# Two interleaved transformer layers on one core: layer B moved to one step behind layer A, lag 2 in place of 3

## The chip, the core and the metric

The kernel runs on one core of a Trainium2 chip. The metric is device time in microseconds (us), the median of the runs. Five engines work side by side, each with its own queue that is worked off in order: PE (TensorE, matmuls, with its weight loads as PEld), DVE (VectorE), ACT (ScalarE), POOL (GpSimd) and SP (SyncE), which here only issues DMAs. Work on different engines is ordered by semaphores: an instruction at the head of a queue that waits holds up everything behind it on that engine.

## The reference

The input x has 2048 rows of 640 values. Four layers follow each other, A B A B, each added to x, each on a layer norm of x. Both A layers share one set of weights, both B layers another.

```python
def _A_ref(x, mem0, Wq, Wk, Wv, Wo, seg_len):      # 32 heads of 192, 64 segments of 32 rows
    mem = mem0                                       # 8 memory rows
    for s in range(n_seg):
        xs = x[:, s * seg_len:(s + 1) * seg_len, :]
        h = jnp.concatenate([mem, xs], axis=1)       # 40 rows
        q = jnp.einsum('btd,dhe->bhte', h, Wq)       # likewise k, v
        scores = jnp.einsum('bhqe,bhke->bhqk', q, k) * scale
        p = _softmax(jnp.where(mask[None, None], scores, -1e9), axis=-1)
        o = jnp.einsum('bhte,hed->btd', jnp.einsum('bhqk,bhke->bhqe', p, v), Wo)
        mem = o[:, :M, :]                            # goes into the next segment
        outs.append(o[:, M:, :])

def _B_ref(x, wqkv, wo):                             # 32 heads of 20, window of 8 at distance 2
    kg = k[:, :, idx_c, :]; vg = v[:, :, idx_c, :]   # rows pos, pos-2, ..., pos-14
    attn = _softmax(jnp.where(mask, jnp.einsum('bhsd,bhswd->bhsw', q, kg) * scale, -1e9))
    return jnp.einsum('bhsw,bhswd->bhsd', attn, vg).reshape(B, S, D) @ wo

x = x + _A_ref(_layernorm(x), A_mem0, ...)
x = x + _B_ref(_layernorm(x), B_wqkv, B_wo)
x = x + _A_ref(_layernorm(x), A_mem0, ...)
x = x + _B_ref(_layernorm(x), B_wqkv, B_wo)
```

Layer A is a recurrence over 64 segments: the memory rows that a segment gives enter the next one. A B segment needs its own 32 rows and the 14 rows before them.

## The kernel before

**Steps and lanes.** The 64 segments are worked in steps. Two lanes lie side by side in every tile: lane 0 is the first A layer on segment t, lane 1 the second A layer on segment t - LAG. Each lane has 40 columns (8 memory, 32 input), so a matmul of layer A has 80 moving columns where both lanes are at work. LAG is 3: steps 0 to 2 have lane 0 alone, steps 3 to 63 both (61 steps), steps 64 to 66 lane 1 alone. In these one-lane steps the matmuls have 40 columns (`set_lanes`, `cols`). Layer B of both lanes runs behind: `step(t)` does the first part of B for b1 = t - 1 (layer norm, K, Q, V and the transposed V) and the second for b2 = t - 2 (scores, P.V, output). So two more steps, 67 and 68, hold B alone. The result of B's lane 0 goes into `xin` and is lane 1's input of the next step; lane 1's goes into `YT` and out.

**A step of layer A.** 32 heads are worked in 8 quads of four heads. For each quad PE projects K (`a_k`, 30 matmuls), Q (`a_q`, 30) and V (`a_v`, 10 matmuls of 384 columns), then P.V of the quad before (`a_pv`, 8), the output projection `a_o` of the quad two before (30 matmuls, added up over all quads in one PSUM tile, `acc`), and the scores (`a_s`, 8). ACT copies K out of PSUM into KF and Kz, takes the exponentials and the reciprocal of the softmax sums (as exp of minus log, tile R). DVE copies Q (QT) and V (Vt, after the P.V that read the old Vt), masks the exponentials (Em) and scales the output of P.V (OT, three instructions, `a_norm`). At the end of a step follow `a_o(5)`, `a_o(6)` and `a_o(7)`; then `mem_out` (DVE) copies the memory columns of acc into hT, the input of the next step's first `a_k`, and `b_x1` forms x1, the input of layer B. Between `a_o(7)` and the next step's first `a_k` stand `b_q` and `b_vt` of layer B (35 matmuls). PSUM gives the projections four buffers in turn (`ps_big`), each free again once its copy is done.

**Weights.** Layer A's weights are 64 pieces of 480 KB ("halves"). They don't fit: 34 stay in SBUF, 30 are read from HBM again in every step, through a ring of six buffers on SP's queue. `half_order` gives the order in which PE needs the halves, `resident_halves` which of them stay (every so-many-th by count). POOL loads layer B's weights (`load_b_weights`), builds its masks at step 1 (`build_masks_b`), expands Q by heads (`b_qexp`, tile QX, against a mask `hmask` of 128x384) and moves x in and the result out.

**What sets the order.** All of `run` but the prologue stands in a block in which the order of the Python calls is the order on every engine. Nothing is rearranged.

Of the kernel before, what the change touches and what calls it, by code (L numbers as in the profile page):

```python
# [10 lines left out]
BF16 = mybir.dt.bfloat16  # L11
F32 = mybir.dt.float32
ACT = mybir.ActivationFunctionType
ALU = mybir.AluOpType
# [3 lines left out]
P = 128  # L18
D = 640
NC = 5  # L20
# [8 lines left out]
LAG = 3  # L29
# [14 lines left out]
def half_order():  # L44

    order = []
    for i in range(NQUAD - 1):
        order += [("k", i), ("q", i), ("v", i)]
        if i >= 2:
            order.append(("o", i - 2))  # L50
    order += [("k", 7), ("q", 7), ("v", 7), ("o", 5), ("o", 6), ("o", 7)]
    return [(kind, i, h) for kind, i in order for h in range(2)]

def resident_halves():
    res = set()
    for n, u in enumerate(half_order()):
        if (n * N_RES) // N_HALVES != ((n + 1) * N_RES) // N_HALVES:
            res.add(u)
    return res

class Kernel:
    def __init__(self, ctx, tc, A_x, A_mem0, A_Wq, A_Wk, A_Wv, A_Wo, B_wqkv, B_wo, out):
        self.tc = tc
        self.nc = tc.nc
# [12 lines left out]
        self.ebp = pool("ebp", 4)  # L77
        self.xp = pool("xio", 1)
# [47 lines left out]
    def load_b_weights(self, i):  # L126
        if i == 0:
            self.nc.gpsimd.dma_start(out=self.wqkv[:].rearrange("p c n -> p (c n)"), in_=self.B_wqkv)
        else:
            self.nc.gpsimd.dma_start(out=self.wo[:].rearrange("p c n -> p (c n)"), in_=self.B_wo)  # L130
# [15 lines left out]
    def build_masks_b(self):  # L146
        nc, cp = self.nc, self.cp

        def band(name, cur):
            m = cp.tile([P, NX], BF16, name=name)  # L150
            nc.gpsimd.memset(m[:], 0.0)
            for half in range(2):
                off = 0 if half == cur else SEG
                for l in range(2):
                    r0 = 64 * half + SEG * l
                    blk = m[r0:r0 + SEG, SEG * l:SEG * (l + 1)]
                    for w in range(BW):
# [14 lines left out]
        hm = cp.tile([P, BHC, NX], BF16, name="hmask")  # L172
        nc.gpsimd.memset(hm[:], 1.0)
        nc.gpsimd.affine_select(out=hm[:], in_=hm[:], compare_op=ALU.is_ge, fill=0.0, base=0,
                                pattern=[[-BD, BHC], [0, NX]], channel_multiplier=1)
        nc.gpsimd.affine_select(out=hm[:], in_=hm[:], compare_op=ALU.is_ge, fill=0.0, base=BD - 1,
                                pattern=[[BD, BHC], [0, NX]], channel_multiplier=-1)
# [33 lines left out]
    def proj(self, kind, i, t):  # L211

        nc = self.nc
        hT = self.hT[t % 2]
        ps = self.big(f"ps_{kind}")
        for n in range(6):
            if n % 3 == 0:
                w = self.half(kind, i, n // 3)
            for c in range(NC):
                nc.tensor.matmul(ps[:, NT * n + self.c0:NT * n + self.c1], lhsT=w[:, c, P * (n % 3):P * (n % 3 + 1)],  # L220
                                 rhs=hT[:, NT * c + self.c0:NT * c + self.c1],
                                 start=(c == 0), stop=(c == NC - 1))
        return ps
# [29 lines left out]
    def a_v_out(self, out):  # L253

        for pr, ps in enumerate(out):
            src = ps[0:NT, 0:384].rearrange("p (j e) -> p j e", j=2)
            dst = self.Vt[0:NT, 512 * pr:512 * (pr + 1)].rearrange("p (j x) -> p j x", j=2)[:, :, 0:DH]
            self.nc.vector.tensor_copy(out=dst, in_=src)  # L258
# [36 lines left out]
    def a_norm(self, i, split=False):  # L295
        nc = self.nc
        ov, r = self.cols(self.ov), self.cols(self.r[:])
        ot = self.ap2.tile([P, 2, 3, NT], BF16, name="OT")
# [14 lines left out]
    def a_o(self, i):  # L313
# [5 lines left out]
        for m in (0, 2, 3, 5, 1, 4):  # L319
            for c in range(NC):  # L320
                nc.tensor.matmul(self.acc[:, NT * c + self.c0:NT * c + self.c1], lhsT=w[m // 3][:, m % 3, P * c:P * (c + 1)], rhs=self.cols(ot[:, m]),  # L321
                                 start=(i == 0 and m == 0 and c == 0), stop=(i == NQUAD - 1 and m == 4), skip_group_check=True)
# [5 lines left out]
    def mem_out(self, t):  # L328
# [6 lines left out]
        nc.vector.tensor_copy(out=h[:, :, self.l0:self.l1, 0:NM], in_=a[:, :, self.l0:self.l1, 0:NM])  # L335
# [98 lines left out]
    def b_qexp(self, c):  # L434
# [3 lines left out]
                                     in1=self.hmask[:, 0:nh, :], op=ALU.mult)  # L438
# [80 lines left out]
    def prologue(self):  # L519
# [9 lines left out]
        self.build_mask_a()  # L529

    def step(self, t):
        T = self.n_seg + LAG
        self.set_lanes(t)
        b1 = t - 1 if 0 <= t - 1 < T else None
        b2 = t - 2 if 0 <= t - 2 < T else None
        nt = t + 1
        a = t < T
        for i in range(NQUAD - 1):
            if a:
                self.a_k(i, t)  # L540
                self.a_q(i, t)
                ps = self.a_v(i, t)
# [3 lines left out]
                if i >= 2:  # L546
                    self.a_o(i - 2)
            if i == 0 and b1 is not None:
                self.b_ln(b1)
            if b2 is not None and 3 <= i <= 4:  # L550
                self.b_pv(i - 3)
            if a and i >= 1:
                self.a_norm(i - 1)
            if b2 is not None and i == 6:
                self.b_wo(b2)
            if b2 is not None:
                if 1 <= i <= 3:
                    self.b_s(b2, 2 * i - 2)
                    self.b_s(b2, 2 * i - 1)
                if i < 3:  # L560
                    self.b_qexp(2 * i)
                    self.b_qexp(2 * i + 1)
                if i == 5:
                    self.b_ot()
            if i == 3 and b1 is not None:
                self.b_ln_apply(b1)
            if a:
                self.a_s()
            if t == 1 and i in (0, 3):
                self.load_b_weights(i)  # L570
            if t == 1 and i == 4:
                self.build_masks_b()
            if i == 1:
                if nt < self.n_seg:
                    self.x_load(nt)
                yseg = t - 3 - LAG
                if yseg >= 0 and yseg % 4 == 3:
                    self.y_store(yseg // 4)
        if a:
            self.a_k(7, t)  # L580
            self.a_q(7, t)
        if nt < T:
            self.ln1_sq(nt)
        if a:
            self.a_pv()
            self.a_v_out(self.a_v(7, t))
            self.a_norm(6, True)
            self.a_s()
            self.a_norm_mid()
            self.a_o(5)  # L590
        if nt < T:
            self.ln1(nt)
        if a:
            self.a_pv()
        if nt < T:
            self.ln1_rstd()
        if a:
            self.a_norm(7)
            self.a_o(6)
        if nt < T:  # L600
            self.ln1_apply(nt)
        if b1 is not None:
            self.b_v(b1)
            self.b_k(b1)
        if a:
            self.a_o(7)
            if nt < T:
                self.mem_out(t)
            self.b_x1(t)
        if b1 is not None:  # L610
            self.b_q(b1)
            self.b_vt()

    def run(self, ctx):
        self.x1p = ctx.enter_context(self.tc.tile_pool(name="x1p", bufs=2))
# [75 lines left out]
```

## Time and profile before

Three runs took 3385.59, 3378.62 and 3387.4 us: the median is 3385.59 us. The profiled execution took 3381.59 us, with a span of 3379.9 us from the first to the last instruction.

| engine | busy us | share of the span | instructions |
|---|---|---|---|
| PE | 3277.7 | 97% | 72896 |
| PEld | 2877.8 | 85% | 72896 |
| DVE | 2179.0 | 64% | 5966 |
| ACT | 1845.1 | 55% | 5830 |
| POOL | 388.5 | 11% | 575 |

The DMA engines are busy in 85% (SP's queue), at 303 GB/s; the chain that ended last is PE to 91%. In the timeline the first `a_k` of a step marks where the step begins:

| stretch | from | to | us each |
|---|---|---|---|
| before step 0 | 0 | 11.15 | |
| step 0 (lane 0, all 64 halves come for the first time) | 11.15 | 89.19 | 78.0 |
| step 1 (lane 0) | 89.19 | 135.46 | 46.3 |
| step 2 (lane 0) | 135.46 | 183.47 | 48.0 |
| steps 3 to 63 (both lanes) | 183.47 | 3209.59 | 49.6 |
| steps 64 to 66 (lane 1) | 3209.59 | 3345.0 | 45.1 |
| steps 67, 68 (B alone) and the last store | 3345.0 | 3379.9 | |

Read the table by stretch: the 61 two-lane steps are 90% of the span, and what is different in them counts 61 times.

### The profile page before, as it was taken

The numbers are of one execution on the slowest core, as the hardware profiler recorded it, in microseconds if no ns is written. First come the engines' busy times: TensorE is split into PE (matmuls) and PEld (weight loads), VectorE is DVE, ScalarE is ACT, GpSimd is POOL, SyncE is SP. The second block draws the span as 40 slices with busy tenths as digits, with TensorE's granted clock in tenths as the row PEclk, the third lists the DMA queues.
The fourth block names the chain that finished last, engine by engine and source line by source line (L and its number), as shares of the span: only waits on it lengthen the run. The fifth ranks groups of instructions, "written<-read, shape, count | busy, mean of one in ns | idle before, by whom it ended". The sixth has DMA issues, their size and how long they took to land.

```text
span 3379.9 us, 164632 instructions
## 1 busy us (share of the span) xinstructions
PE 3277.7 (97%) x72896; PEld 2877.8 (85%) x72896; DVE 2179.0 (64%) x5966; ACT 1845.1 (55%) x5830; POOL 388.5 (11%) x575
## 2 busy tenths in 40 slices
PE   6899999999999999999999999999999999999987
PEld 4788888888888888888888888888888888888875
DVE  2566666666666666666666666666666666666665
ACT  2455555555555555555555555555555555555543
POOL 0210111011011011101101101110110110111011
PEclk8999999999999999999999999999999999999998
DMA  9988988888888888898888889888988888888894
GB/s 394 359 296 300 309 300 300 309 299 297 302 306 298 299 306 300 300 312 294 302 302 308 297 301 311 299 299 306 306 300 297 305 296 298 309 298 304 300 337 161
DMA packets 298412, 1023.87 MB, mean 303 GB/s; under 512 B 34288, under 2 KB 34288, under 8 KB 297568
## 3 DMA queue, kind: packets, MB, share of 16 engines
q1 hardware_dynamic: 294624, 1004.85, 85.4%
q8 instruction: 570, 9.34, 1.1%
q0 software_dynamic: 3072, 8.48, 0.8%
q14 instruction: 146, 1.20, 0.1%
HBM read 1010.58 MB, written 2.62 MB: 300 GB/s over the span
## 4 chain that ended last, share of the span: by engine, by line
PE 91%; DVE 4%; DMA 3%; issue 1%; POOL 0%; ACT 0%; SPq 0%; POOLq 0%; ACTq 0%
PE ps_v L249 25%; PE ps_k L220 16%; PE ps_q L220 16%; PE ps_acc L321 14%; PE ps_o L286 5%; PE ps_s L267 2%; PE ps_s L268 2%; PE ps_bq L405 2%; PE ps_bk L405 2%; PE ps_bs L445 2%; PE ps_bv L405 1%; PE ps_by L488 1%; DMA w_q<-in_A_Wq_dram 1%; DVE Vt L258 1%; DMA w_ring<-in_A_Wq_dram 1%
## 5 line engine op out<-in xcount | busy, mean ns | idle before, releaser
L290 ACT ACTIVATE R<-ps_o 64x160 f32<-64x160 f32 (+1 forms) x2144 | 627.4, 293 | 926.0 <-issue 512.6
L258 DVE CAST Vt<-ps_v 80x384 bf16<-80x384 f32 x1072 | 557.8, 550 | 402.2 <-PE ps_o L286 331.7
L249 PEld LDWEIGHTS <-hT 128*128 128x128 bf16 x5360 | 494.6, 99 | 293.9 <-issue 13.9
L437 POOL TENSOR_TENSOR QX<-QB,hmask 128x384 bf16<-128x384 bf16 (+1 forms) x402 | 326.2, 832 | 2801.6 <-ACT QB L416 2159.4
L220 PEld LDWEIGHTS <-w_ring 128*128 128x128 bf16 x15075 | 597.1, 100 | 19.0 <-issue 8.7
L249 PE MATMUL ps_v<-w_ring,hT 128*128 128x384 bf16 x2680 | 529.4, 329 | 5.0 <-DMA w_ring<-in_A_Wv_dram 4.9
L249 PE MATMUL ps_v<-w_v,hT 128*128 128x384 bf16 x2680 | 530.6, 329 | 2.4 <-DMA w_v<-in_A_Wv_dram 2.4
L321 PE MATMUL ps_acc<-OT,w_o 128*128 128x80 bf16 (+1 forms) x9045 | 482.5, 200 | 6.6 <-issue 5.2
L238 DVE CAST QT<-ps_q 128x480 bf16<-128x480 f32 (+1 forms) x536 | 340.6, 635 | 226.6 <-PE ps_q L220 208.6
L301 DVE TENSOR_TENSOR OT<-ps_o,R 128x320 bf16<-128x320 f32 (+1 forms) x536 | 254.7, 475 | 318.3 <-ACT R L292 314.2
L220 PE MATMUL ps_q<-hT,w_q 128*128 128x80 bf16 (+1 forms) x9045 | 406.0, 200 | 7.4 <-DMA w_q<-in_A_Wq_dram 4.9
L321 PE MATMUL ps_acc<-OT,w_ring 128*128 128x80 bf16 (+1 forms) x7035 | 399.9, 200 | 2.0 <-DMA w_ring<-in_A_Wo_dram 2.0
L321 PEld LDWEIGHTS <-w_o 128*128 128x128 bf16 x9045 | 381.0, 99 | 7.5 <-issue 5.7
L220 PE MATMUL ps_k<-hT,w_ring 128*128 128x80 bf16 (+1 forms) x8040 | 369.7, 200 | 5.9 <-DMA w_ring<-in_A_Wk_dram 2.6
L220 PE MATMUL ps_k<-hT,w_k 128*128 128x80 bf16 (+1 forms) x8040 | 370.2, 200 | 3.1 <-DMA w_k<-in_A_Wk_dram 2.0
L220 PEld LDWEIGHTS <-w_q 128*128 128x128 bf16 x9045 | 351.3, 100 | 9.0 <-DMA w_q<-in_A_Wq_dram 5.8
L220 PE MATMUL ps_q<-hT,w_ring 128*128 128x80 bf16 (+1 forms) x7035 | 324.8, 200 | 9.7 <-issue 5.0
L220 PEld LDWEIGHTS <-w_k 128*128 128x128 bf16 x8040 | 315.7, 100 | 4.0 <-DMA w_k<-in_A_Wk_dram 2.4
L321 PEld LDWEIGHTS <-w_ring 128*128 128x128 bf16 x7035 | 306.6, 99 | 2.3 <-DMA w_ring<-in_A_Wo_dram 2.3
L231 ACT CAST KF<-ps_k 128x320 bf16<-128x320 f32 (+1 forms) x536 | 220.0, 410 | 160.4 <-PE ps_k L220 159.6
L286 PEld LDWEIGHTS <-Vt 80*128 80x128 bf16 x4288 | 208.9, 98 | 73.4 <-DVE OT L311 20.4
L292 ACT ACTIVATE R<-R 128x320 f32<-128x320 f32 (+1 forms) x536 | 245.7, 458 | 16.9
(94 smaller groups left out, 4049.3 us busy)
## 6 DMA issues: line engine op xcount, KB each, us to landing
w_ring<-in_A_Wk_dram SPq DMA_DIRECT2D x536, 480.0 KB, 5.1
w_ring<-in_A_Wv_dram SPq DMA_DIRECT2D x536, 480.0 KB, 5.0
w_ring<-in_A_Wq_dram SPq DMA_DIRECT2D x469, 480.0 KB, 5.0
w_ring<-in_A_Wo_dram SPq DMA_DIRECT2D x469, 480.0 KB, 5.3
w_q<-in_A_Wq_dram SPq DMA_DIRECT2D x9, 480.0 KB, 9.6
w_o<-in_A_Wo_dram SPq DMA_DIRECT2D x9, 480.0 KB, 9.7
w_k<-in_A_Wk_dram SPq DMA_DIRECT2D x8, 480.0 KB, 9.6
w_v<-in_A_Wv_dram SPq DMA_DIRECT2D x8, 480.0 KB, 9.6
```

Of the source, the lines that this page charges most:

```text
L220: nc.tensor.matmul(ps[:, NT * n + self.c0:NT * n + self.c1], lhsT=w[:, c, P * (n % 3):P * (n % 3 + 1)], rhs=hT[:, NT * c + self.c0:NT * c ...
L231: nc.scalar.copy(out=kf, in_=pv[:, :, 0:3:2, :])
L238: self.nc.vector.tensor_copy(out=self.cols(qt[:]), in_=self.cols(ps[:, 0:6 * NT].rearrange("p (a n) -> p a n", a=6)))
L249: nc.tensor.matmul(ps[:, 0:384], lhsT=hT[:, NT * c:NT * c + P], rhs=w[:, c, :], start=(c == 0), stop=(c == NC - 1))
L258: self.nc.vector.tensor_copy(out=dst, in_=src)
L286: nc.tensor.matmul(self.cols(ov[:, pr, k]), lhsT=vt[0:NT, 512 * pr + c0:512 * pr + c0 + P], rhs=self.cols(em[0:NT, 2 * pr + k // 2]), star ...
L290: nc.scalar.activation(out=self.cols(r[r0:r0 + 64, :, j]), in_=self.cols(src), func=ACT.Ln)
L292: nc.scalar.activation(out=rf, in_=rf, func=ACT.Exp, scale=-1.0)
L301: nc.vector.tensor_tensor(out=oc[:, :, 0:3:2], in0=ov[:, :, 0:4:3], in1=r, op=ALU.mult)
L321: nc.tensor.matmul(self.acc[:, NT * c + self.c0:NT * c + self.c1], lhsT=w[m // 3][:, m % 3, P * c:P * (c + 1)], rhs=self.cols(ot[:, m]), s ...
L405: nc.tensor.matmul(ps[:, NX * n:NX * (n + 1)], lhsT=self.wqkv[:, c, e0:e0 + P], rhs=self.h2T[:, c, :], start=(c == 0), stop=(c == NC - 1))
L437: self.nc.gpsimd.tensor_tensor(out=qx[:, 0:nh, :], in0=self.qb[:, c, :].unsqueeze(1).to_broadcast([P, nh, NX]), in1=self.hmask[:, 0:nh, :] ...
```

## The change

- LAG is 2. Steps 0, 1 and 64, 65 have one lane, steps 2 to 63 both (62 steps); there are 66 A steps, and one step (66) with B alone.
- Layer B runs for one b = t - 1 within step t: layer norm at quad 0, Q and K at 1, V at 2, the transposed V at 3, P.V at 4 and 5, transpose and output at 6; the scores at quads 2 to 4. Nothing of B is left between `a_o(7)` and the next step's first `a_k`.
- The output projection of a quad is four quads behind (OLAG = 4) in place of two: `a_o(i - 4)` from quad 4 on, and `a_o(3)` to `a_o(7)` at the end of the step. OT has four buffers.
- In quad 7 the P.V of quad 6 stands between K and Q (it stood behind Q), and one of the two copies of V goes to ACT.
- The last output projection ends chunk by chunk (all of a 128-row chunk of the output before the next), `mem_out` is two copies (chunks 0 and 1, then 2 to 4), and the first K of a step takes chunk after chunk of its input.
- Which halves stay is chosen by the columns that PE works between them; 34 stay, 30 are read again.
- `wqkv` is loaded after quad 6 of step 0, `wo` after quad 0 of step 1 (each behind a copy of one element of Em, so that the DMA can't start earlier). The masks of B are built in the prologue. `hmask` is 128x6 and is read with a step of 0 along the columns.

```diff
-LAG = 3
+LAG = 2
+OLAG = 4
...
 def resident_halves():
+    order = half_order()
+    whole = sum(n for _, n in order)
+    streamed, at = 0, 0
     res = set()
-    for n, u in enumerate(half_order()):
-        if (n * N_RES) // N_HALVES != ((n + 1) * N_RES) // N_HALVES:
+    for u, n in order:
+        if streamed < N_HALVES - N_RES and at * (N_HALVES - N_RES) >= streamed * whole:
+            streamed += 1
+        else:
             res.add(u)
+        at += n
     return res
...
+    def load_b_weights(self, w, src):
+        self.nc.gpsimd.tensor_copy(out=w[0:1, 0, 0:1], in_=self.em[0:1, 0, 0:1])
+        self.nc.gpsimd.dma_start(out=w[:].rearrange("p c n -> p (c n)"), in_=src)
...
     def proj(self, kind, i, t):
+        w = [self.half(kind, i, h) for h in range(2)]
+        mem_last = kind == "k" and i == 0
+        order = [(n, c) for c in range(NC) for n in range(6)] if mem_last else [(n, c) for n in range(6) for c in range(NC)]
+        for n, c in order:
...
     def a_o(self, i):
+        order = [(m, c) for m in (0, 2, 3, 5, 1, 4) for c in range(NC)]
+        if i == NQUAD - 1:
+            order = [(m, c) for m in (0, 2, 3) for c in range(NC)] + [(m, c) for c in range(NC) for m in (5, 1, 4)]
...
     def mem_out(self, t):
-        nc.vector.tensor_copy(out=h[:, :, self.l0:self.l1, 0:NM], in_=a[:, :, self.l0:self.l1, 0:NM])
+        for cs in (slice(0, 2), slice(2, NC)):
+            nc.vector.tensor_copy(out=h[:, cs, self.l0:self.l1, 0:NM], in_=a[:, cs, self.l0:self.l1, 0:NM])
...
     def b_qexp(self, c):
-                                     in1=self.hmask[:, 0:nh, :], op=ALU.mult)
+                                     in1=self.hmask[:, 0:nh].unsqueeze(2).to_broadcast([P, nh, NX]), op=ALU.mult)
...
     def step(self, t):
-        b1 = t - 1 if 0 <= t - 1 < T else None
-        b2 = t - 2 if 0 <= t - 2 < T else None
+        b = t - 1 if t >= 1 else None
...
+            if b is not None and i == 6:
+                self.b_ot()
+            if a:
                 ps = self.a_v(i, t)
                 if i >= 1:
                     self.a_pv()
                 self.a_v_out(ps)
+            if b is not None:
+                if i == 0:
+                    self.b_ln(b)
+                if i == 1:
+                    self.b_q(b)
+                    self.b_k(b)
+                if i == 2:
+                    self.b_v(b)
+                if i == 3:
+                    self.b_vt()
+                if 4 <= i <= 5:
+                    self.b_pv(i - 4)
+            if a and i >= OLAG:
+                self.a_o(i - OLAG)
             if a and i >= 1:
                 self.a_norm(i - 1)
+            if b is not None:
                 if 1 <= i <= 3:
+                    self.b_qexp(2 * i - 2)
+                    self.b_qexp(2 * i - 1)
+                if 2 <= i <= 4:
+                    self.b_s(b, 2 * i - 4)
+                    self.b_s(b, 2 * i - 3)
             if a:
                 self.a_s()
+            if b is not None and i == 0:
+                self.b_ln_apply(b)
+            if b is not None and i == 6:
+                self.b_wo(b)
...
+        self.a_k(7, t)
+        self.a_pv()
+        self.a_q(7, t)
         if nt < T:
             self.ln1_sq(nt)
+        self.a_v_out(self.a_v(7, t), act=True)
+        self.a_norm(6)
+        self.a_s()
+        self.a_o(7 - OLAG)
         if nt < T:
             self.ln1(nt)
+        self.a_pv()
         if nt < T:
             self.ln1_rstd()
+        self.a_norm(7)
+        for i in range(8 - OLAG, 7):
+            self.a_o(i)
         if nt < T:
             self.ln1_apply(nt)
+        self.a_o(7)
+        if nt < T:
+            self.mem_out(t)
+        self.b_x1(t)
...
-            for t in range(self.n_seg + LAG + 2):
+            for t in range(self.n_seg + LAG + 1):
```

More of the change, by code (lines that the diff above doesn't have):

```diff
@@ L318, in a_o @@
         w = [self.half("o", i, h) for h in range(2)]
[L319 to L322, printed above, removed]
+        order = [(m, c) for m in (0, 2, 3, 5, 1, 4) for c in range(NC)]
+        if i == NQUAD - 1:
+            order = [(m, c) for m in (0, 2, 3) for c in range(NC)] + [(m, c) for c in range(NC) for m in (5, 1, 4)]
+        for m, c in order:
+            nc.tensor.matmul(self.acc[:, NT * c + self.c0:NT * c + self.c1], lhsT=w[m // 3][:, m % 3, P * c:P * (c + 1)], rhs=self.cols(ot[:, m]),
+                             start=(i == 0 and m == 0 and c == 0), stop=(i == NQUAD - 1 and m == 4), skip_group_check=True)
     def lanes(self, flat):
@@ L529, in prologue @@
         self.build_mask_a()
+        self.build_masks_b()
     def step(self, t):
```

106 lines of the change are left out of this document (30 added, 76 removed).

## The prediction

> **What bounds the kernel now.** I read the page first (who is busy, the chain), then PE's waits in the two-lane steps, then the timeline of one such step and of the end.
>
> ```profile
> PE 3277.7 (97%) x72896; PEld 2877.8 (85%) x72896; DVE 2179.0 (64%) x5966; ACT 1845.1 (55%) x5830; POOL 388.5 (11%) x575
> PEclk8999999999999999999999999999999999999998
> PE 91%; DVE 4%; DMA 3%; issue 1%; POOL 0%; ACT 0%; SPq 0%; POOLq 0%; ACTq 0%
> ```
>
> PE sets the time, at the full granted clock in all but the first and last slice. DVE and ACT have a third and more of the span free, so they can matter only by being late at one place. PE's waits between 233.8 and 3209 us:
>
> ```profile
> PE ps_o L286 <- DVE OT L311: 11.8, 60, 0.2
> PE ps_bq L405 <- issue: 6.0, 11, 1.6
> ```
>
> No DMA stands in that list: the ring keeps up. Per step there is one wait of 0.20, for the P.V of quad 7. The busy time by stretch shows what a one-lane step is:
>
> ```profile
> 137.00:185.00 48.00, 41.74 (x1104) 35.52 (x1104) 27.18 (x88) 22.13 (x88) 5.71 (x9) 1.00 0.86 311
> 2010.00:2059.40 49.40, 49.20 (x1095) 43.58 (x1092) 32.91 (x89) 28.06 (x87) 5.38 (x7) 1.00 0.89 303
> 3250.00:3300.00 50.00, 44.48 (x1216) 38.27 (x1213) 29.51 (x98) 23.74 (x94) 5.70 (x8) 1.00 0.88 323
> ```
>
> The columns after the width are PE, PEld, DVE, ACT, POOL, clock, DMA share, GB/s. Half the columns save a one-lane step only some 4 us: its matmuls come every 0.025 us, not every 0.036, but V's 384 columns stay, and PE has more gaps. So a one-lane step costs nearly as much as a two-lane one. The timeline of PE in a two-lane step:
>
> ```profile
> 2016.77 1.24 PE L321 MATMUL ps_acc<-OT,w_o 128*128 128x80 bf16 x30
> 2017.84 1.04 PE L405 MATMUL ps_bq<-h2T,wqkv_sb 128*128 128x64 bf16 x30
> 2018.72 0.44 PE L428 MATMUL ps_bvt<-ident,VTB 128*128 128x128 bf16 x5
> 2019.00 0.70 PE L220 MATMUL ps_k<-hT,w_ring 128*128 128x80 bf16 x15
> 2027.13 0.45 PE L286 MATMUL ps_o<-Em,Vt 80*128 80x80 bf16 x8
> 2028.08 0.70 PE L220 MATMUL ps_k<-hT,w_ring 128*128 128x80 bf16 x15
> 2054.67 0.45 PE L286 MATMUL ps_o<-Em,Vt 80*128 80x80 bf16 x8
> ```
>
> and DVE's side of it:
>
> ```profile
> 2018.05 0.24 DVE L335 CAST hT<-ps_acc 128x80 bf16<-128x80 f32 x1 [0.30 <-PE ps_acc L321]
> 2055.02 1.02 DVE L258 CAST Vt<-ps_v 80x384 bf16<-80x384 f32 x2 [1.11 <-PE ps_o L286]
> 2057.65 0.33 DVE L311 TENSOR_TENSOR OT<-ps_o,R 64x160 bf16<-64x160 f32 x1
> 2058.01 0.33 DVE L494 TENSOR_TENSOR xin<-ps_by,x 128x160 bf16<-128x160 f32 x1
> ```
>
> Between `a_o(7)` and the next K lie 1.16 us of layer B (2017.84 to 2019.00), and behind them DVE's copy of the memory columns is hidden.
>
> **The sum, part by part.** All against the profiled execution, span 3379.9.
>
> *Steps.* A clean two-lane step takes 49.34 (from 2010.32 to 2059.66, the same V of two steps); the mean of the 61 is 49.61, of which 0.27 are scattered gaps ("issue" among them). One-lane steps took 46.3 and 48.0 early, 45.1 late. The change takes away one early and one late and adds a two-lane one: 49.6 - 47.2 - 45.1 = -42.7.
>
> *The end.* The last `a_o` ends at 3344.0, the span 35.9 later: two B passes, the second from 3356.57. Now there is one. From the rows of the end: x1, its square and the statistics 1.3, mean and variance 0.75, logarithm and exponential 0.65, two scalings 0.6, so h2T after 3.3; then Q in 1.8 (30 matmuls at the 54 ns apiece of 3356.57, where the clock has dropped) and its copy 0.5. QX starts at +5.7, not +16.7. From QX's start (3360.65) to the last YT (3371.52) were 10.9; V stands ahead of the scores, +0.25; the store and the end take 8.4 as before. Sum 25.2, so -10.7.
>
> So -53 without new waits. What stands against that is paid 64 times.
>
> *The step's boundary.* B's 1.16 us of cover are gone. In row 2016.77 the last matmul starts at 2016.77 + 29 x 0.0357 = 2017.81; the copy starts 0.24 later (2018.05). The smaller first copy takes about 0.19 (128x80 took 0.24, 128x40 0.20), and PE follows DVE after 0.05 (the OT row before the P.V of quad 7). K could start 0.48 after that last matmul, in place of 0.04: wait 0.44. This takes the copy to wait for all thirty matmuls. In the built program it does: the thirty report once, by the last, and the first copy waits for that count. So the chunk order of `a_o(7)` hides nothing, and only the second copy is covered (K's third chunk comes 0.43 after its start). If the copy could start after the second chunk, nine matmuls earlier, the wait would be 0.13: that is the other end, 20 us for all steps. The Trainium skill's "PSUM — Partial Sum Buffer", section "PSUM bank collisions raise a hardware error", speaks against the change here: it has PSUM guarded by bank and not by address, and all five chunks of acc are one bank. By that rule the larger wait holds; before, no copy ran beside such matmuls, so the trace can't show it.
>
> *Quad 3.* After the P.V of quad 2 come the transposes (0.28) and a score matmul of B (0.165); the next takes the PSUM buffer that the first copy of V must leave. That copy starts 0.35 after the P.V's start and takes 0.55 (2054.67, 2055.02), so with 0.05 the matmul can go at +0.95, and PE is there at 0.29 + 0.28 + 0.165 = 0.735: wait 0.21. The same wait is seen in the trace where it is small: P.V at 2027.13, K at 2028.08, +0.95, where PE was there at +0.90; that 0.05 goes. The next K finds the second V copy at +1.42, having come at +1.40: 0.02.
>
> *Quad 6.* P.V of quad 6 moves ahead of Q (1.08). Its Em comes behind OT on DVE: P.V of quad 5 at 2054.67, OT done so that the next instruction starts at 2058.01, +3.34; Em takes 0.31, so +3.70 with PE's 0.05. PE is there at 0.29 + 1.08 (`a_o`) + 0.28 (scores) + 0.73 (`b_wo`) + 1.08 (K) = 3.46: wait 0.24. Before, xin and YT came first on DVE, but Q covered them too.
>
> *Quad 7.* The wait of 0.20 goes. Em is now behind ACT's copy of V, at most 0.55 as on DVE, at least 0.41 like ACT's 128x320 copy; at 0.48 Em is there 0.25 before PE. Price 0.
>
> Per step: 0.44 + 0.21 + 0.02 + 0.24 - 0.20 - 0.05 = +0.66. One-lane steps come out alike (+0.7). Bounds: -0.25 (all three hidden) and about +0.9 (nothing of the old waits gone). Some of the 0.27 of scattered gaps, 11 of them at `b_q`, should fall into the new waits: I take 0.07 off.
>
> *Priced at nothing.* POOL's masks (17.5 us at 91 to 109) and wqkv: step 0 is bound by the DMAs (share 1.02 to 1.03), the bytes up to its end are the same. QX with a zero step: its wait for scores and QB leaves 5 us of room. The streamed halves: worked with the rows above, the time from a ring buffer coming free to its next use is at least 7.0 us (7.7 before), a landing takes 5.1. Queue of SP: as many issues a step. B's ACT copies in quads 1 and 2: the tightest (VTB before the next Q) has 0.13 left. Step 1 now holds all of B: 49 in place of 46.3; against the 47.2 above that is +1.8.
>
> Sum: -42.7 + 1.8 - 10.7 + 64 x 0.59 = -13.8; span 3366, execution 3368. The median of the three runs lies 4.0 above the profiled execution, so 3368 to 3372: I say **3371**. A change below 0.3% (10 us) can't be told from none here: the bound is at 3375.4.
>
> **The rivals.**
> 1. *The new waits are hidden or much smaller* (the copy starts early, or the scattered gaps fall into them entirely). For it: gaps of 0.27 a step that have slack to give. Against it: the +0.95 pattern is in the trace to 0.01. With 0.1 to 0.3 a step: 3340 to 3355.
> 2. *No measurable difference.* 0.1 a step more than I have, or 4 us less at the end, and the gain is below 0.3%: 3376 to 3387.
> 3. *Slower: QX becomes the bound.* POOL takes 0.91 us for a QX of 128x384 against a full mask; with the zero step it is unknown. Two of them must fit between QB (2.4 after the P.V of quad 0) and the score matmul 7.0 after it: up to 2.3 us each nothing happens, beyond it PE waits for four times the excess in every step. At 2.6 us it is over 1 us a step: 3400 and above. Against it: before, one of the two operands was already read with a zero step (over heads).
> 4. *The lag isn't shortened in effect*: excluded, the loop has two turns fewer.
>
> **How the numbers follow.** Forecast case 3362 to 3380: 0.5, of which 0.35 below 3375.4. Rival 1: 0.22. Rival 2 outside that: 0.13. Rival 3: 0.15. Faster 0.35 + 0.22 = 0.57, same 0.15 + 0.13 = 0.28, slower 0.15. The range takes in most of rival 1 and the upper bound (+0.9 a step gives 3389): 3345 to 3390.
>
> **What would show it.** In the waits, 64 times each: K of quad 0 for DVE's hT with 0.4, B's score matmul for Vt with 0.2, P.V for Em with 0.24, and none of 0.20 for OT. Steps of 50.2 us. The end 25 us after the last `a_o`. Wrong it would be with steps under 49.8 or over 50.6, with QX above 2.3 us, or with waits for the ring.

## The result, and the profile after

The changed kernel takes 3366.4 us (median of 5 runs, 3364.0 to 3374.4) against 3381.8 us for the kernel before (median of 5, 3378.6 to 3387.4): ratio 0.9955, 95% interval 0.9939 to 0.9971, 0.45% faster. The profiled execution took 3363.99 us with a span of 3362.3, against a forecast span of 3366.

The lines of the page that answer to those shown of before (who is busy, the clock, the chain):

```profile
PE 3259.2 (97%) x71808; PEld 2849.6 (85%) x71808; DVE 2111.4 (63%) x5880; ACT 1836.7 (55%) x5809; POOL 356.8 (11%) x569
PEclk7999999999999999999999999999999999999998
PE 88%; DVE 4%; ACT 3%; DMA 2%; issue 2%; POOL 0%; POOLq 0%; SPq 0%; DVEq 0%
```

PE is still the bound, at the full clock. It issues 1088 matmuls fewer, yet the chain holds more of ACT: PE now waits in more places. PE's waits in the two-lane steps of after (138 to 3244 us; engine, tile and line, whom it waited for: total us, times, longest):

```profile
PE ps_k L230 <- DVE hT L351: 17.2, 61, 0.3
PE ps_acc L336 <- issue: 3.7, 5, 1.4
PE ps_v L259 <- issue: 2.5, 4, 1.1
PE ps_q L230 <- issue: 2.4, 7, 0.8
```

The wait for OT that led the list of before is gone; in its place K waits in every step for the memory copy. The two other waits that were forecast are not in this list, although they are there: the view counts idle time from the modelled end of the matmul before, about 0.2 us after its start, while matmuls follow one another every 0.036 us. So the wait at the boundary, 0.46 from start to start, is listed as 0.28, and those of 0.23 and 0.26 are not listed at all. PE's weight loads have a list of their own, and it shows both, once in each of the 62 steps and with what they wait for:

```profile
PEld L461 <- DVE Vt L271: 21.1, 62, 0.3
PEld L299 <- DVE Em L286: 13.9, 62, 0.2
```

What a wait costs PE has to be read from start to start, in the timeline. PE's side of an undisturbed step of after (start, duration, line, operation; rows left out between):

```profile
675.55 0.45 PE L299 MATMUL ps_o<-Em,Vt 80*128 80x80 bf16 x8
679.27 0.46 PE L299 MATMUL ps_o<-Em,Vt 80*128 80x80 bf16 x8
687.43 1.24 PE L336 MATMUL ps_acc<-OT,w_o 128*128 128x80 bf16 x30
688.96 0.27 PE L230 MATMUL ps_k<-hT,w_ring 128*128 128x80 bf16 x3 [0.28 <-DVE hT L351]
708.88 0.45 PE L444 MATMUL ps_bvt<-ident,VTB 128*128 128x128 bf16 x5
709.16 0.73 PE L461 MATMUL ps_bs<-QX,KB 128*128 128x384 bf16 x2
710.01 1.24 PE L230 MATMUL ps_k<-hT,w_ring 128*128 128x80 bf16 x30
```

- Boundary: 30 matmuls from 687.43 end their issue at 688.50; K starts at 688.96. Loss 0.46 (listed as 0.28).
- Quad 3: the two score matmuls from 709.16 should take 0.33 and the eight of layer A's scores 0.285, so K was due at 709.78; it starts at 710.01. Loss 0.23. The 0.73 of the two score matmuls (0.49 where nothing stops them) shows where it lies.
- Quad 6: from P.V to P.V 3.72, where the work between makes 3.46. Loss 0.26.

Where the time went, profiled execution against profiled execution (step starts are the starts of the first K):

| stretch | before | after | difference |
|---|---|---|---|
| up to step 1 | 89.2 | 89.9 | +0.7 |
| early one-lane steps | 2: 94.3 | 1: 47.8 | -46.5 |
| two-lane steps | 61 x 49.61 = 3026.1 | 62 x 50.12 = 3107.2 | +81.0 |
| late one-lane steps, to the end of the last `a_o` | 3: 134.4 | 2: 91.5 | -43.0 |
| behind it | 35.9 | 26.0 | -9.9 |
| span | 3379.9 | 3362.3 | -17.6 |

An undisturbed two-lane step takes 49.87 (49.34 before), so 0.25 of the mean are scattered gaps (0.27 before).

### The profile page after: what moved, and what is told of

The parts are those of the page before. It is cut to its first block, busy times and chain, and to the rows that moved or that the text cites. A ratio compares the mean times of both kernels' runs of the same rounds, so it can differ in the third digit from the quotient of the medians.

```text
span 3362.3 us, 162172 instructions
## 1 busy us (share of the span) xinstructions
PE 3259.2 (97%) x71808; PEld 2849.6 (85%) x71808; DVE 2111.4 (63%) x5880; ACT 1836.7 (55%) x5809; POOL 356.8 (11%) x569
## 4 chain that ended last, share of the span: by engine, by line
PE 88%; DVE 4%; ACT 3%; DMA 2%; issue 2%; POOL 0%; POOLq 0%; SPq 0%; DVEq 0%
PE ps_v L259 25%; PE ps_q L230 17%; PE ps_k L230 15%; PE ps_acc L336 15%; PE ps_o L299 5%; ACT R L303 2%; PE ps_s L281 2%; PE ps_s L280 2%; PE ps_bq L421 2%; PE ps_bk L421 2%; PE ps_bs L461 2%; PE ps_bv L421 1%; PE ps_st L363 1%; DVE Vt L271 1%; DMA w_q<-in_A_Wq_dram 1%
## 5 line engine op out<-in xcount | busy, mean ns | idle before, releaser
L271 DVE CAST Vt<-ps_v 80x384 bf16<-80x384 f32 x990 | 513.0, 550 | 396.4 <-PE ps_o L299 363.3
L230 PE MATMUL ps_q<-hT,w_q 128*128 128x80 bf16 (+1 forms) x13860 | 578.6, 201 | 9.3 <-DMA w_q<-in_A_Wq_dram 5.6
L230 PEld LDWEIGHTS <-w_ring 128*128 128x128 bf16 x12870 | 509.4, 100 | 36.4 <-issue 31.1
L230 PEld LDWEIGHTS <-w_q 128*128 128x128 bf16 x13860 | 523.8, 100 | 11.5 <-DMA w_q<-in_A_Wq_dram 6.5
L230 PE MATMUL ps_k<-hT,w_ring 128*128 128x80 bf16 (+1 forms) x10890 | 489.2, 201 | 25.0 <-DVE hT L351 18.4
L336 PEld LDWEIGHTS <-w_ring 128*128 128x128 bf16 x8910 | 351.5, 100 | 8.2 <-DMA w_ring<-in_A_Wo_dram 7.2
L336 PE MATMUL ps_acc<-OT,w_o 128*128 128x80 bf16 (+1 forms) x6930 | 323.2, 201 | 10.0 <-issue 6.9
L336 PEld LDWEIGHTS <-w_o 128*128 128x128 bf16 x6930 | 275.3, 100 | 11.5 <-issue 8.1
L230 PE MATMUL ps_k<-hT,w_k 128*128 128x80 bf16 (+1 forms) x4950 | 246.5, 201 | 1.2 <-DMA w_k<-in_A_Wk_dram 0.9
L299 PE MATMUL ps_o<-Em,Vt 80*128 80x80 bf16 (+1 forms) x4224 | 237.1, 199 | 5.8
L286 DVE TENSOR_TENSOR Em<-E,maskA 80x320 bf16<-80x320 bf16 (+1 forms) x528 | 166.8, 316 | 97.0 <-ACT E L283 82.0
```

Of the source, the lines that this page charges most:

```text
L299: nc.tensor.matmul(self.cols(ov[:, pr, k]), lhsT=vt[0:NT, 512 * pr + c0:512 * pr + c0 + P], rhs=self.cols(em[0:NT, 2 * pr + k // 2]), star ...
```

## The experiments

The theory: steps and the end give 53 us, and three new waits (0.46 at the boundary, 0.23 in quad 3, 0.26 in quad 6), each with its own cause and place, take most of it back. The rivals: the chunk order hides the boundary; a wait only moves when its cause is removed; the lag itself, the weights' new order or some load on PE costs the time. The kernels ran in three groups, each beside the kernel before on the same chip; the changed kernel's row is that of the result. The median of the kernel before lies between 3379.7 and 3383.2 in all of them. "Undisturbed" is the commonest length of a two-lane step in the profiled execution; between 27 (segment columns first) and 61 (less traffic) of a kernel's 61 or 62 two-lane steps have it to 0.02 us.

| kernel | median us | ratio to before (95%) | undisturbed step | mean two-lane step |
|---|---|---|---|---|
| changed kernel | 3366.4 | 0.9955 (0.9939 to 0.9971) | 49.87 | 50.12 |
| plain order at the boundary | 3371.8 | 0.9975 (0.9962 to 0.9988) | 49.93 | 50.31 |
| transposes early | 3359.5 | 0.9935 (0.9919 to 0.9951) | 49.69 | 49.98 |
| P.V 6 inside Q 7 | 3353.1 | 0.9914 (0.9899 to 0.9929) | 49.61 | 49.95 |
| segment columns first | 3377.0 | 0.9982 (0.9966 to 0.9999) | 49.75 | 50.38 |
| both moves | 3344.3 | 0.9887 (0.9872 to 0.9902) | 49.43 | 49.81 |
| P.V 6 behind Q 7 | 3364.9 | 0.9945 (0.9928 to 0.9962) | 49.82 | 50.19 |
| projections 3 quads behind | 3368.2 | 0.9956 (0.9941 to 0.9971) | 50.04 | 50.18 |
| lag 3 | 3409.2 | 1.0075 (1.0059 to 1.0091) | 49.87 | 50.07 |
| less traffic | 3322.0 | 0.9828 (0.9812 to 0.9843) | 49.88 | 49.88 |
| less traffic, segment columns first | 3314.8 | 0.9804 (0.9789 to 0.9819) | 49.75 | 49.76 |
| streamed halves by count | 3365.1 | 0.9959 (0.9942 to 0.9975) | 49.88 | 50.13 |
| both moves, 35 resident halves, 5 buffers | 3337.7 | 0.9865 (0.9836 to 0.9893) | 49.42 | 49.63 |

### The boundary in its plain order

```
-        mem_last = kind == "k" and i == 0
+        mem_last = False
...
-        if i == NQUAD - 1:
-            order = [(m, c) for m in (0, 2, 3) ...] + [(m, c) for c in range(NC) for m in (5, 1, 4)]
...
-        for cs in (slice(0, 2), slice(2, NC)):
+        for cs in (slice(0, NC),):
```

> The changed kernel with the last output projection and the first K in their plain order and the memory copied in one piece. Theory (the chunk order hides nothing, because the copy starts only when the last of the 30 matmuls has reported; predicted boundary wait 0.44 us): the wait grows only by the longer copy of 80 columns instead of 32, some 0.05 to 0.1 us a step, 3 to 6 us in all: 3367 to 3373, and the gap between the last output projection's start and K's start grows from 1.53 to about 1.6 us. Rival (chunk by chunk the copy overlaps a good part of the projection): the wait grows by 0.3 us or more a step, 19 us or more: 3385 or above.

The boundary of that kernel:

```profile
591.36 1.24 PE L334 MATMUL ps_acc<-OT,w_o 128*128 128x80 bf16 x30
592.64 0.24 DVE L349 CAST hT<-ps_acc 128x80 bf16<-128x80 f32 x1 [0.84 <-PE ps_acc L334]
592.93 0.70 PE L230 MATMUL ps_k<-hT,w_ring 128*128 128x80 bf16 x15 [0.33 <-DVE hT L349]
```

From the projection's start to K's it is 1.57 us, 1.53 in the changed kernel. The undisturbed step grows by 0.06 to 49.93: 3.7 us over 62 steps, and the median by 5.4, although the intervals of the two ratios overlap. The copy starts 1.28 after the projection's start in both (592.64 here, 688.71 against 687.43 there). So the reordering of the last projection brings nothing, and that of K only the difference between a short copy and a long one. The Trainium skill's "PSUM — Partial Sum Buffer", section "PSUM bank collisions raise a hardware error", says that a write and a read by two engines may not meet in one bank; here the copy of two finished chunks does not start before the last matmul of the bank, at +1.28 as a copy of all five. The built program makes it wait, so that no run shows what the bank would do.

### The wait of quad 3

```
-                if i == 3:
-                    self.b_vt()
...
+            if b is not None and i == 3:
+                self.b_vt()            # ahead of a_v, where b_ot stands in quad 6
```

> The transposes of layer B's V moved from behind the P.V of quad 3 to ahead of its V, nothing else. Theory (the second score matmul of layer B and the K behind it wait for a ps_big buffer that a V copy frees, 0.23 us a step): with one buffer less taken behind P.V the next K meets the first V copy instead of the second, about 0.05 us of the wait stays, 0.18 us of 62 to 64 steps go: 11 to 12 us less than the changed kernel, 3354 to 3356. Rival (the gap only moves, to the scores, which wait for Q's copy on VectorE behind the transposes' copies, or to the P.V of the next quad): the time stays within 3 us of 3366.

Quad 3 of that kernel:

```profile
460.21 0.45 PE L299 MATMUL ps_o<-Em,Vt 80*128 80x80 bf16 x8
460.50 0.49 PE L461 MATMUL ps_bs<-QX,KB 128*128 128x384 bf16 x2
461.17 1.24 PE L230 MATMUL ps_k<-hT,w_ring 128*128 128x80 bf16 x30
```

The two score matmuls are 0.49 long again, not 0.73, and K comes 0.96 behind P.V where the work makes 0.91: the 0.05 that was to stay stays. The undisturbed step is 49.69, the 0.18 less that the theory gave. The median fell by 7 us, not 11, and the intervals of the ratios overlap, so the evidence here is the step and not the time; the scattered gaps of the profiled execution are 0.29 a step, 0.25 in the changed kernel.

### The wait of quad 6

```
-        self.a_k(7, t)
-        self.a_pv()
-        self.a_q(7, t)
+        self.a_k(7, t)
+        self.a_q(7, t, 10, self.a_pv)   # proj calls a_pv ahead of its matmul 10
```

> The P.V of quad 6 moved from ahead of quad 7's Q into it, behind its first 10 of 30 matmuls (0.36 us), nothing else. Theory (P.V waits 0.26 us for Em): the wait is covered, 0.26 us of 62 to 64 steps go, 16 us: 3350. Rival (the chain through R, OT and Em of quad 7 does not get earlier, so that the P.V of quad 7 waits as it did in the kernel before): what quad 6 gains quad 7 loses, 3363 to 3369, and a wait for Em stands ahead of the P.V of quad 7.

Quads 6 and 7 of that kernel:

```profile
1124.34 0.45 PE L301 MATMUL ps_o<-Em,Vt 80*128 80x80 bf16 x8
1127.80 0.52 PE L232 MATMUL ps_q<-hT,w_q 128*128 128x80 bf16 x10
1128.15 0.46 PE L301 MATMUL ps_o<-Em,Vt 80*128 80x80 bf16 x8
1132.30 0.31 PE L365 MATMUL ps_st<-sq,ones 128*128 128x64 bf16 x5
1132.44 0.45 PE L301 MATMUL ps_o<-Em,Vt 80*128 80x80 bf16 x8
```

The P.V of quad 6 starts the moment its ten Q matmuls are out (1127.80 + 10 x 0.0357 = 1128.16), and that of quad 7 follows the statistics with no gap. Undisturbed step 49.61, 0.26 less; time 13 us less, of 16.

### P.V of quad 6 behind the whole Q

```
         self.a_k(7, t)
-        self.a_pv()
         self.a_q(7, t)
+        self.a_pv()
```

> The P.V of quad 6 put back where the kernel before had it, behind the whole Q of quad 7; VectorE's and ScalarE's work as in the changed kernel. Theory: the 0.26 us ahead of quad 6's P.V go, but the chain P.V, R, OT, Em of VectorE starts 0.8 us later and puts about 0.24 us ahead of the P.V of quad 7: net nothing, 3363 to 3370. Rival (the old wait at quad 7's P.V came from VectorE copying both halves of V, and ScalarE's copy has cured it): 16 us less, 3350.

The tail of quad 7 in that kernel:

```profile
586.67 0.32 DVE L286 TENSOR_TENSOR Em<-E,maskA 80x320 bf16<-80x320 bf16 x1
586.71 0.31 PE L363 MATMUL ps_st<-sq,ones 128*128 128x64 bf16 x5
587.05 0.46 PE L299 MATMUL ps_o<-Em,Vt 80*128 80x80 bf16 x8
```

P.V was due at 586.86 and comes at 587.05, right behind Em: 0.19 lost there for 0.26 won at quad 6. Undisturbed step 49.82, the time the same as that of the changed kernel. So ScalarE's copy of V does not cure the old wait, 0.36 in the kernel before, by itself: 0.19 of it comes back when the chain of OT starts later. The rest of the 0.36 can be ScalarE's copy or one more change at this place: in the kernel before, two of OT's three instructions stood behind Em on DVE, and now all three stand ahead of it. No run undoes that alone. Of the places tried, only the one in the middle of Q avoids both waits.

### Both moves together

> The two moves together: the transposes ahead of quad 3's V, the P.V of quad 6 inside quad 7's Q. Theory (the three waits stand at three places and are independent): an undisturbed two-lane step comes to 49.87 - 0.18 - 0.26 = 49.43 us, and the time to 3366 - 0.44 x 62 = 3339, up to 3347 if gaps of PE's issue take part of it back as they did with the first move alone. Rival (one of the waits comes back once the other is gone): the undisturbed step stays at 49.6 or above and the time at 3353 or above.

3344.3 us, undisturbed step 49.43: exactly 49.87 - 0.18 - 0.26. In PE's weight loads the two rows of waits for Vt and Em are gone. PE's own work in a step, its 1088 matmuls each at the usual interval of its shape, is 48.9; the boundary's 0.46 and the 0.05 left in quad 3 make 49.4. With that an undisturbed step is accounted for, and the waits of quads 3 and 6 are shown to be independent of each other.

### Projections three quads behind

```
-OLAG = 4
+OLAG = 3
```

The same constant gives OT's buffers, now three, and enters the choice of the halves that stay.

> Output projections three quads behind their P.V, not four. Theory: behind the P.V of quad 7 stand then two projections (0.29 + 2 x 1.075 = 2.44 us) where the first norm of OT is ready 2.84 us after that P.V's start: PE waits 0.40 us more a step for OT, 25 us: 3388 to 3395. Rival (the lag is not needed, the norm is ready in time or the wait only takes the place of the one for the memory copy): 3366 to 3370.

Quad 3 and the last projections of a step of that kernel:

```profile
662.31 0.45 PE L444 MATMUL ps_bvt<-ident,VTB 128*128 128x128 bf16 x5
662.59 1.24 PE L336 MATMUL ps_acc<-OT,w_ring 128*128 128x80 bf16 x30
663.66 0.49 PE L461 MATMUL ps_bs<-QX,KB 128*128 128x384 bf16 x2
...
688.07 0.45 PE L299 MATMUL ps_o<-Em,Vt 80*128 80x80 bf16 x8
690.91 1.24 PE L336 MATMUL ps_acc<-OT,w_o 128*128 128x80 bf16 x30 [0.24 <-DVE OT L314]
```

The wait for OT is as forecast: 2.84 from P.V to `a_o(7)`, where P.V and two projections make 2.44, so 0.40. But the step grew by 0.17 only, since a projection now stands in quad 3 between the transposes and the scores and covers the 0.23 there (0.40 - 0.23 = 0.17). My expectation had left that out. So of the 0.40 that the lag of four quads saves at the end it spends 0.23 in quad 3. The time, 3368.2, can't be told from that of the changed kernel: the 0.17 would be 10 us, but the scattered gaps of the profiled execution are 0.14 a step here, 0.25 there.

### The lag put back to 3

```
-LAG = 2
+LAG = 3
-        self.xin = pers("xin", [P, 2, NC, SEG], 2)
+        self.xin = pers("xin", [P, 2, NC, SEG], 3)     # and its indices % 3
```

> The changed kernel with the second segment's lag put back to 3 (a third buffer for the step's input), everything else as changed. Theory: one more early step with one lane (47.8 us), one more late one (45.8), one less with two (50.1): 43.5 us more, 3406 to 3414, slower than the kernel before, because the new order's waits stay. Rival (the lag of 2 itself costs part of the 0.5 us a step, by work that it squeezes between layer B's end and the next step's input): the undisturbed two-lane step falls clearly under 49.87 us, and the time stays under 3400.

3409.2 us, 43 more than the changed kernel, and the undisturbed step is 49.87 to the hundredth. So the lag costs nothing in a step, it is worth one one-lane step at each end less a two-lane one, and without it the new order is slower than the kernel before.

### The streamed halves by count

```
-        if streamed < N_HALVES - N_RES and at * (N_HALVES - N_RES) >= streamed * whole:
+        if (n * N_RES) // N_HALVES != ((n + 1) * N_RES) // N_HALVES:     # the rule of before
```

> The changed kernel with the streamed halves chosen by equal counts, as the kernel before chose them, not by equal spacing in PE's time. Theory (this part was priced at nothing, since the loads lead by more than they take to land in either case): an undisturbed two-lane step stays at 49.87 us, the time within 6 us of 3366. Rival (it was the even spacing that kept the ring ahead of the denser end of the step, with four projections in a row): PE waits for ring tiles at those projections, 0.3 us or more a step, 3385 or above.

3365.1 us, undisturbed step 49.88: no difference. The price of nothing was right.

### The boundary covered: segment columns first

K's 64 columns of segment tokens need no memory. Of the first 12 matmuls these columns go first, then their 16 memory columns, then the other 18 matmuls whole.

```
...
+            for cs in (slice(NM, LT), slice(0, NM)):
+                for n, c in order[:12]:
+                    nc.tensor.matmul(pv[:, n, :, cs], lhsT=..., rhs=hv[:, c, :, cs], ...)
+            order = order[12:]
```

> The first 12 matmuls of the step's first K are cut in two: first their 64 columns of segment tokens, which need no memory, then their 16 columns of memory tokens, then the other 18 as before. Theory (PE waits 0.46 us a step for the memory copy and for nothing else at this place): the 12 early matmuls of some 0.03 us each cover about 0.37 us of it; the 12 extra ones cost 0.2 to 0.3 us; net 0.1 to 0.2 us a step less, 6 to 12 us: 3354 to 3360; the wait ahead of the memory columns is left at about 0.1 us. Rival (the segment columns come late too, or PE's loss there is the turn from the projection to K and not the copy): no gain, and the extra matmuls cost 0.2 us a step or more: 3379 or above.

The boundary of that kernel, with DVE's copy (rows left out between):

```profile
1296.59 1.24 PE L344 MATMUL ps_acc<-OT,w_o 128*128 128x80 bf16 x30
1297.66 0.25 PE L234 MATMUL ps_k<-hT,w_ring 128*128 128x64 bf16 x3
1297.87 0.30 DVE L359 CAST hT<-ps_acc 128x32 bf16<-128x32 f32 x2 [0.85 <-PE ps_acc L344]
1298.11 0.22 PE L234 MATMUL ps_k<-hT,w_ring 128*128 128x16 bf16 x3
1298.41 0.27 PE L238 MATMUL ps_k<-hT,w_ring 128*128 128x80 bf16 x3
```

K starts 1.07 behind the projection, with no gap; the 12 early matmuls take 0.36 (0.030 each), the copy lies beside them, and 0.09 of the wait is left. The extra 12 of 16 columns take 0.30 (0.025 each). The undisturbed step is 49.75, 0.12 less, as the theory said. But the median is 10.6 us more, where the theory had 6 to 12 less. The twelve runs lie between 3365.1 and 3390.4, three of them under the changed kernel's median, and the intervals of the ratios just overlap: what is clear is that the gain did not come. What grew are the scattered gaps, from 0.25 to 0.63 a step in the profiled execution, which with 3384.8 us is a long one of the twelve. PE's waits in the two-lane steps of this kernel, the longest:

```profile
PE ps_q L238 <- issue: 16.6, 19, 2.5
PE ps_k L238 <- issue: 3.0, 8, 0.6
PE ps_k L234 <- issue: 2.4, 3, 1.2
```

"Issue" is time in which PE waited for nothing that the view shows. Its place gives it away. With all of PE's instructions (matmuls, weight loads and 200 to 270 semaphore instructions) counted in order of start, the instruction behind such a gap is number 193 of a block of 256: 57 times out of the 321 intervals above 0.25 us in this kernel, 40 of 333 in the changed one, while no other position comes more than 5 times. With the semaphore instructions left out of the count the pattern is lost. The page's list of DMA queues shows what a block is (queue and kind: packets, MB, share of 16 engines), here for the changed kernel:

```profile
q1 hardware_dynamic: 290304, 990.10, 86.2%
q8 instruction: 562, 9.21, 1.1%
```

562 packets of 16,384 bytes, one for 256 instructions of 64 bytes: PE's 143,821 instructions fill 562 such blocks. In this kernel's DMA records no block is used sooner than 1.2 us after its transfer ended (the median is 3.0), and at all of the 40 gaps but one it was 1.2 to 1.6. Their transfers took no longer than others (mean 1.00 us, median of all 0.99) but began late: 3.3 us after the first use of the block before, where the median is 1.8. The Trainium skill's "Runtime: NRT & Kernel Launch", section "Instruction fetch mechanics", has such blocks (16 KiB, 256 instructions, fetched by the engine's own DMA queue) and calls the cost of crossing into one "mostly hidden". Here 40 of 561 crossings are not hidden in the changed kernel: these intervals sum to 32 us of its span, half of it outside the two-lane steps, where matmuls of 40 columns use up a block faster, and to 54 us with the segment columns first. Two of the gaps there, of 2.1 us, were followed by 3.4 us at a granted clock of 0.5 (from 246.0 and from 1805.9 us on), up to 1.7 us more each; the changed kernel's two-lane steps have no such stretch.

### The same with less traffic

If the blocks come late because they stand behind the weights, less weight traffic cures it. Where the half h=1 is streamed, its load is left out and the tile of the half before is used.

```
+        if h == 1 and not res:
+            return self.last[:].rearrange("p (a b) -> p a b", a=3 if kind == "o" else NC)
...
+        self.last = t_
```

> The changed kernel without the second half of those streamed weights whose half h=1 is not resident: 12 of the 30 streamed halves of a step are not loaded, and the matmuls use the tile of the half before in their place, so the output is not the reference's; every matmul, copy and wait on the engines stays. Theory (PE's scattered gaps are blocks of 256 of its instructions, 16 KB each, that the instruction queue begins to fetch too late behind the weights): with 40% less traffic the late blocks all but go; in two-lane steps the gaps at block edges fall from 14 us to under 3, the mean two-lane step from 50.1 to 49.9 or less, while the undisturbed one stays 49.87; with the late blocks and weight waits of the one-lane steps (some 20 us) and the shorter first step (12 halves, some 15 us) 3366 comes to 3310 to 3325. Rival (the gaps come from the rate at which PE takes instructions, or from something inside PE, and not from traffic): the mean two-lane step stays above 50.05 us.

> The same 12 halves not loaded (output not the reference's), in the kernel whose first K takes the segment columns of 12 matmuls ahead of their memory columns. Theory (that order saves 0.12 us in each undisturbed step and lost it, and more, to late instruction blocks): without late blocks it is faster than the kernel with less traffic alone, by 5 to 8 us, with a two-lane mean of about 49.8 us. Rival (the extra matmuls cost PE's time in a way that the undisturbed steps do not show): it stays slower than that kernel, by up to 10 us.

PE's waits in the two-lane steps, first with less traffic alone, complete:

```profile
PE ps_k L233 <- DVE hT L354: 17.2, 61, 0.3
```

then with the segment columns first, complete too:

```profile
PE ps_v L270 <- issue: 0.5, 1, 0.5
```

The scattered gaps are gone: the mean two-lane step is the undisturbed one (49.88, and 49.76 against 49.75). Transfers of blocks begin 0.46 us after the first use of the block before (median of the two-lane steps with less traffic alone; 1.8 with all the weights). The order that won nothing with the full traffic now wins 7.1 us (3322.0 to 3314.8, each of its four runs below each of the other's four), as its undisturbed step says. So the gaps are late instruction blocks, and what makes them late is the weights' traffic. How the queues share an engine these runs don't show, nor why twelve matmuls more on some 1090 a step more than double the gaps of the profiled execution; that short matmuls use a block up sooner, and that a step without waits gives the fetch no time to catch up, is only argued. The second would fit the kernel with the longest undisturbed step (50.04), which has the smallest gaps of those with the full traffic, 0.14 a step; but the next longest (49.93) has 0.38.

### A version that beats both

Both moves, one more resident half, one ring buffer fewer.

```
-N_RES = 34
-RING = 6
+N_RES = 35
+RING = 5
```

> The two moves together (transposes ahead of quad 3's V, P.V of quad 6 inside quad 7's Q), and one more resident half for one ring buffer less: 29 streamed halves a step, not 30. Theory of the late blocks: 3% less traffic saves 1 to 2 us of them, 3342 to 3344. Rival: five ring buffers lead by 1.7 us less (one load in 29 of a 50 us step), and PE waits for weights in most steps: 3355 or above.

PE's waits in its two-lane steps:

```profile
PE ps_k L232 <- DVE hT L353: 17.4, 62, 0.3
PE ps_k L232 <- DMA w_ring<-in_A_Wk_dram: 3.2, 4, 0.8
PE ps_v L261 <- issue: 2.2, 2, 1.6
PE ps_q L232 <- issue: 1.5, 4, 0.5
```

3337.7 us, ratio to before 0.9865 (0.9836 to 0.9893), clear of the changed kernel's 0.9955 (0.9939 to 0.9971). Against both moves alone (0.9887, 0.9872 to 0.9902) 1 to 2 us were expected and 6.6 came, but the intervals overlap. The undisturbed step is the same; what is less are the gaps in the profiled execution, 0.21 a step for 0.38, and a few waits for weights have come (3.2 us). The rival was wrong: five buffers do.

## Why the prediction was right

- *Steps.* The forecast for the steps gone and added was -42.7, with step 1 at +1.8 and two late steps at +0.59 each: -39.7. Measured: -46.5 - 43.0 + 49.6 = -39.9 (step 1 took 47.8, not 49, the late ones 45.8, not 45.7). That it is the lag which buys it, the lag-3 kernel shows, with 43 us more.
- *The end.* 26.0 us where 25.2 was forecast.
- *The three new waits* were sized well: boundary 0.46 (forecast 0.44), quad 3 0.23 (0.23), quad 6 0.26 (0.24); those of quads 3 (but for 0.05) and 6 went with their causes, each in an experiment of its own, and the boundary's fell to 0.09 where columns that don't need the copy went first. The argument that the chunk order hides nothing held to 0.06 us a step.
- *The term that was mis-sized* is the old wait ahead of the P.V of quad 7, set at 0.20 from the list of waits. It was worth 0.36. In the kernel before:

```profile
2013.28 0.31 PE L347 MATMUL ps_st<-sq,ones 128*128 128x64 bf16 x5
2013.41 0.33 DVE L311 TENSOR_TENSOR OT<-ps_o,R 64x160 bf16<-64x160 f32 x1
2013.79 0.46 PE L286 MATMUL ps_o<-Em,Vt 80*128 80x80 bf16 x8 [0.20 <-DVE OT L311]
```

  Five matmuls of 64 columns are issued in 0.147 us, so P.V was due at 2013.43 and lost 0.36; the list counts from the modelled end, 2013.59. (The Trainium skill's "Perfetto Trace Analysis", section "Per-instruction lifecycle: what the profiler-reported window actually captures", says that the profiler estimates a TensorE instruction's end; these rows show by how much an estimate of that kind shortens a wait.) With 0.36 the step's sum is 0.44 + 0.23 + 0.24 - 0.36 - 0.05 = +0.50; measured undisturbed +0.53, forecast +0.66.
- *Scattered gaps* were to fall by 0.07 a step into the new waits; they fell by 0.02. They are late instruction blocks in the kernel before too (27 intervals above 0.25 us at position 193 sum to 16 us of its 61 two-lane steps), so a wait elsewhere need not take them up. The mean step grew by 0.51, forecast 0.59. That 0.08 over 62 steps, 5 us, is about what the forecast was high by. The old wait was set 0.16 too low and the fall of the gaps 0.05 too high; these errors have opposite signs, so that part of the nearness is luck.
- *Rival 1* (copy starts early) was false in its cause: plain order costs 5 us, not 20. *Rival 2* was missed by little: 10 us is the bound, 15.4 came. *Rival 3* (QX on POOL becomes the bound) did not come, by a row of after's groups:

```profile
L453 POOL TENSOR_TENSOR QX<-QB,hmask 128x384 bf16<-128x384 bf16 (+1 forms) x396 | 295.7, 766 | 2863.2 <-ACT QB L432 2470.7
```

  Its mean over both shapes is 766 ns, 832 before; for 128x384 alone it is 839, 913 before, far under the 2.3 us that were allowed. That the zero step made it faster is likely, but no run changes it alone.
- *Priced at nothing* was right for the streamed halves; the move of layer B's weights and masks was not tried alone, and up to step 1 the kernels differ by 0.7 us.

## What to carry to other kernels

A shorter pipeline buys whole steps at its ends and pays in every step between, so count the waits that the tighter order creates, place by place, start to start; here they gave back 31 us (62 x 0.51) of 49, and two of the three could be removed by moving five transposes and eight matmuls to where the buffer or the operand was ready. A wait that only fills when other work stands in front of it is best met by splitting a long group of matmuls around it. And before covering the last wait of a step, look at whether the instruction stream can keep up: with some 2200 instructions per 50 us and the DMA engines 86% busy, a gain of 0.12 us a step did not come, and with less traffic it did.

## What the runs showed of the hardware that I had not expected

- PE's instructions come by DMA in blocks of 256, 16 KB each, and with the weights' traffic at 300 GB/s over the span some blocks come late: 32 us of gaps in 3362. With 12 of 30 streamed halves left out (187 GB/s) the same program has 3 us of them.
- A QX of 128x384 with a zero step in its second operand took 839 ns in the changed kernel, one from a full mask 913 in the kernel before.
- A matmul of 16 columns with its weight load takes 0.025 us, the same as one of 40; one of 64 takes 0.030 and one of 80 0.036.
- After some gaps of PE of about 2 us the granted clock fell to 0.5 for 3.4 us, and V's matmuls came every 0.32 us in place of 0.16; after others of the same length it did not.
